# First batch of a fused attention and SwiGLU kernel: other pieces, other queues and an earlier place for q

## The chip, the cores and the metric

The kernel runs on one core of one Trainium2 chip. The metric is the device time of one execution in microseconds. TensorE (PE) multiplies matrices, VectorE (DVE), ScalarE (ACT) and GpSimd (POOL) work on elements, SyncE (SP) issues transfers. Each engine executes its instructions in the order in which the program gives them; engines wait for each other, and for transfers, through semaphores. Transfers are issued on three queues here: SP's and ACT's (called hardware queues below, q1 and q10 in the profile) and POOL's (q0), the only one that casts float32 to bfloat16 under way. All three are served by the same 16 DMA engines.

## The reference

Inputs are q, k and v of 8 batches, 8 heads, 576 tokens and 64 features, in float32, and the weights of a gated feed-forward layer.

```python
kv = np.einsum('bhsd,bhse->bhde', k, v)          # 64x64 per batch and head
out = np.einsum('bhsd,bhde->bhse', q, kv)
rms = np.sqrt(np.mean(out * out, axis=-1, keepdims=True) + 1e-06)
attn = out / rms * g_norm                         # norm over the 64 features of a head
x = attn.transpose(0, 2, 1, 3).reshape(4608, 512)
xn = x / np.sqrt(np.mean(x * x, axis=-1, keepdims=True) + 1e-06) * rms_g
g = xn @ w_gate                                   # 512 -> 1536
y = (g * sigmoid(g) * (xn @ w_val)) @ w_out       # 1536 -> 512
```

The attention is linear: there is no softmax, and k times v is summed over all tokens before q comes in. So no row of the result can be made before all of k and v of its heads has arrived, but a part of q's tokens suffices for a part of the rows.

## The kernel before, in words

Each batch gives a main part of 512 tokens, in 4 chunks of 128, and 64 remaining tokens; the remainders of all 8 batches form a ninth group of 512 rows. For each group the feed-forward layer makes 12 gate blocks (`gate_of`, weights `wg`) and 12 value blocks (`val_of`, weights `wv`) of 128 features, each of four matmuls (L694, for the very first three gates L722), takes silu of the gate on ACT (L703), multiplies it with the value on DVE (L712), and then multiplies by the output weights `wo` (L729). Heads are worked in four pairs j; `P0` is pairs 0 and 1, `P1` pairs 2 and 3. While PE does the feed-forward layer of one group, the attention of the next is placed between its blocks by a planner (`Placer`), which counts a cost per engine and slot.

The first batch has nothing to lie under, so it is written out by hand (L824 to L895), and its 512 rows are split in two halves: chunks 0 and 1, the leading half of q, and chunks 2 and 3, the late half. Tokens lie on partitions, four adjacent tokens to a partition. In order:

- POOL issues v's remainder and v in two halves of 4 heads (L824, L825), with a cast, and then the eight weight blocks `wg0`, `wv0` to `wg3`, `wv3` (L842).
- SP issues k's first 4 heads and the leading half of q, ACT k's other heads and k's remainder (L826 to L830). Since a partition holds four adjacent tokens of 64 features, k goes in pieces of 1024 bytes and half of q in pieces of 512. The late half of q follows on both queues (L836 to L838), held by a dependency until v's remainder has landed.
- DVE and ACT cast k and the leading q to bfloat16 (L856 to L859); PE runs matmuls on zeros meanwhile (`spin`).
- PE multiplies k and v of pairs 0 and 1 (`kv_pairs`, L297), transposes the leading q in eight 128x128 matmuls (`qT_mm`, L316), multiplies k and v of pairs 2 and 3; DVE masks the products into `kvs` (`kv_pairs_out`, L304); `qT_out` (L338) copies the transposed q.
- PE multiplies `kvs` by the transposed q (`oT_mm`, L423), ACT squares that (`sqT_`, L434), PE sums the squares (`stat_pairs`, L448), and forms the same product in the other orientation (`o_pairs`, L390).
- `lead_chain` (L482) turns the sums into one factor per token and head on DVE, with a square root on ACT, after which it loads ACT's table for Silu (L498). DVE multiplies (`xna_pairs`, L400), PE transposes the outcome (`xT_mm`, L571), and ACT and DVE copy it with the gain into x (`xT_out`, L581 and L583).
- Then come the early blocks (`early`, L910 to L913): on the leading half alone, 256 columns to a matmul, gates of weight block 0, its values, gates and values of block 1, and so on. `behind(n)` (L918) puts the late half's steps behind early block n: transposes behind 0, products and squares behind 2 and 3, statistics behind 5, normalisation behind 11 and 12, transposes into x behind 14 and 15. POOL casts the late half.
- `cut` (L987) says where the first three pairs of gate and value on the second half are put in: before, behind the gates of the last weight block.

Three pools of PSUM buffers bind this order: `mm1` (3 buffers), `o2` (2) and `att` (3). An operation that takes the next buffer of a pool waits until the readers of the buffer's last use are done.

Batch 0's rows are stored by `store` (L743), one transfer for each chunk of 128 rows as `rows_of` (L733) lays them out.

Of the kernel before, what the change touches and what calls it, by code (L numbers as in the profile page):

```python
# [87 lines left out]
def kernel(  # L88
# [112 lines left out]

    def two(t):
        return src[t][0, :, MAIN:S, :].rearrange("h (p c) d -> p h (c d)", c=2)
# [46 lines left out]
    class Att:  # L250
# [61 lines left out]
        def qT_mm(self, js, chunks, pool=None):  # L312
            qT_ps = (pool or att_p).tile([128, len(js), len(chunks) * 128], BF16, name="o2" if pool else "att")
            for n, j in enumerate(js):
                for i, c in enumerate(chunks):
                    nc.tensor.matmul(  # L316
                        qT_ps[:, n, i * 128 : (i + 1) * 128], lhsT=self.pair(0, c, j), rhs=ident, is_transpose=True,
                        start=True, stop=True, skip_group_check=True,
                    )
            return qT_ps  # L320
# [161 lines left out]
        def lead_chain(self, c0, c1, guard=False):  # L482
# [8 lines left out]
            V.reciprocal(out=r, in_=u)  # L491
# [6 lines left out]
            nc.scalar.preload_act_table(ACT.Silu)  # L498
            V.reciprocal(out=al, in_=nt)
# [233 lines left out]
    def rows_of(g, t):  # L733

        if g < B:
# [105 lines left out]
    make_identity(nc, identf)  # L841
    w_loads = [load_w(n) for n in range(len(FB))]  # L842
    G.memset(kvs[0], 0.0)
    G.memset(kvs[1], 0.0)
    for tile_ in (kc[0], kc[1], vc[0], vc[1]):
        G.memset(tile_[REM:, :, NC * D :], 0.0)
# [7 lines left out]
    spin(mm1_p.tile([128, MAIN], FP32, name="mm1"), 18)  # L854
# [9 lines left out]
    kvb = a.kv_pairs(P1)  # L864
    for i, j in enumerate(P0):
        a.kv_pairs_out(kva, i, j)
    a.qT_out(qa, P0, 0, A)
    a.qT_out(qb, P1, 0, V)
# [12 lines left out]
    for i, j in enumerate(P1):  # L881
        a.sqT_(a.oT_mm((j,), 0, 2, (o2_p, mm1_p)[i], 4 * (1 - i)), (j,), 0, 2)
    a.stat_pairs(P0, 0, 2, mm1_p, "mm1", guard=True)
    a.stat_pairs(P1, 0, 2, mm1_p, "mm1")
    ox = a.o_pairs(P0, 0, 2, att_p, "att")
    oy = a.o_pairs(P1, 0, 2, att_p, "att")
    a.lead_chain(0, 2)
    spin(mm1_p.tile([128, MAIN], FP32, name="mm1"), 5)
    for o, js in ((ox, P0), (oy, P1)):
        for i, j in enumerate(js):  # L890
            a.xna_pairs(o[:, :, 2 * i : 2 * i + 2], (j,), 0, 2)

    for j, pool_, eng in zip(ALL, (o2_p, o2_p, None, None), (A, V, A, V)):
        a.xT_mm((j,), (0, 1), pool_)
        a.xT_out(j, (0, 1), eng)  # L895

    for hsx in (H0, H1):
        cast_main(0, 0, G, hsx, cs=(2, 4))
    for t in (0, 2, 1):
        load_cast(1, t, (0, H))  # L900
        if t:
            load_cast(1, t)
    wo_loads = [load_wo(n) for n in range(NF // OB)]
# [12 lines left out]
    steps = {5: (0, 4), 7: (4, 6), 8: (6, 8), 9: (8, 12)}  # L916

    def behind(n):  # L918
        if n == 0:
            ps = a.qT_mm(ALL, (2, 3))  # L920
            a.qT_out(ps[:, 0:2], P0, 2, V)
            a.qT_out(ps[:, 2:4], P1, 2, V)
        elif n in (2, 3):
            js = (P0, P1)[n - 2]
            a.sqT_(a.oT_mm(js, 2, 4, o2_p), js, 2, 4)
        elif n == 5:
# [6 lines left out]
        if n in (7, 8):  # L933
            held[n - 7] = a.o_pairs((P0, P1)[n - 7], 2, 4, att_p, "att")
        if n in (11, 12):
            i = (11, 12).index(n)
            a.xna_pairs(held[i], (P0, P1)[i], 2, 4)
        elif n in (14, 15):
            i = (14, 15).index(n)
# [47 lines left out]
    cut = len(early) - FB[-1]  # L987
# [37 lines left out]
```

## Time and profile before

| | |
|---|---|
| times of three runs | 321.53, 321.70, 322.65 us; median 321.7 |
| profiled execution | 321.76 us |
| its span | 320.0 us, 5497 instructions, granted clock 1.00 |
| PE busy | 312.8 us (98%) |
| DVE, ACT, POOL busy | 169.2, 138.0, 85.2 us |
| moved | 40.69 MB, mean 127 GB/s |
| first matmul on k and v | 10.43 us |
| first gate matmul | 17.54 us |
| first value matmul | 19.30 us |
| first matmul on the output weights | 43.03 us |

The page says for each engine how long it was busy, and names the chain of work that ended last, followed backwards from the last instruction. A queue row gives packets, MB and the time that the packets took as a share of the 16 engines' time; it can be over 100%, since packets overlap. A timeline row gives the start and the duration in us, then engine, line, operation, tile written and tile read, shapes and a count of merged instructions; in brackets stands how long the engine had been idle before, and what ended that. PEld is PE's load of the stationary operand. Sizes of casting transfers are counted as written, after the cast.

### The profile page before, as it was taken

To read this page: it belongs to the slowest core of one execution; us is meant where nothing else is said; L and a number is where in the kernel's file an instruction comes from. 1 tells how busy PE (TensorE), PEld (TensorE's weight loads), DVE (VectorE), ACT (ScalarE), POOL (GpSimd) and SP (SyncE) were. 2 spreads that over 40 slices of the span, in tenths; PEclk is the share of its full clock that TensorE was granted. 3 is DMA by queue.
4 is the path that set the end of the run, shared out by engine and by line. 5 is a ranking of instruction groups with operands and counts; after the bars stand their busy time and mean duration, and the time that the engine had idled before them with its cause. 6 is when DMAs were issued, how large, how long until landed. Compare 5 with 4: busy or idle time off the path is not lost.

```text
span 320.0 us, 5497 instructions
## 1 busy us (share of the span) xinstructions
PE 312.8 (98%) x2122; PEld 157.7 (49%) x2122; DVE 169.2 (53%) x381; ACT 138.0 (43%) x254; POOL 85.2 (27%) x105
## 2 busy tenths in 40 slices
PE   8799999999999999999999999999999999999995
PEld 3578865444444444444544444444444444444443
DVE  4565536589749651955186717571778043203410
ACT  1465454596667314632383228322842233223321
POOL 8653430077017400830075007500510000000000
PEclk9999999999999999999999999999999999999999
DMA  8999999999761974498349875964000600040002
GB/s 210 221 203 199 195 231 205 228 209 135 153 197 53 166 155 137 131 166 153 121 128 133 148 153 145 153 127 137 11 3 10 183 21 2 15 107 12 0 33 98
DMA packets 79253, 40.69 MB, mean 127 GB/s; under 512 B 42872, under 2 KB 74748, under 8 KB 79228
## 3 DMA queue, kind: packets, MB, share of 16 engines
q0 software_dynamic: 31200, 14.22, 35.1%
q1 hardware_dynamic: 46544, 25.14, 32.2%
q10 hardware_dynamic: 1484, 0.99, 1.0%
q8 instruction: 16, 0.26, 0.3%
q14 instruction: 9, 0.07, 0.1%
HBM read 37.78 MB, written 9.44 MB: 148 GB/s over the span
## 4 chain that ended last, share of the span: by engine, by line
PE 91%; DMA 8%; issue 0%; DVE 0%; ACT 0%; POOLq 0%
PE mm L694 57%; PE o L729 27%; DMA wv<-in_moe_w_val_dram 5%; DMA remv<-in_v_dram 2%; PE att L281 2%; PE mm L729 2%; PE o L375 1%; PE att L375 0%; PE att L362 0%; PE mm L756 0%; PE o L756 0%; PE att L571 0%; PE att L327 0%; PE att L423 0%; PE att L350 0%
## 5 line engine op out<-in xcount | busy, mean ns | idle before, releaser
L712 DVE TENSOR_TENSOR h<-silu,mm 128x512 bf16<-128x512 bf16 (+1 forms) x120 | 75.5, 631 | 86.9 <-PE mm L694 77.0
L703 ACT ACTIVATE silu<-mm 128x512 bf16<-128x512 f32 (+1 forms) x120 | 66.4, 556 | 86.4 <-PE mm L694 75.3
L694 PE MATMUL mm<-x,wv 128*128 128x512 bf16 (+1 forms) x432 | 99.9, 356 | 0.2 <-DMA wv<-in_moe_w_val_dram 0.2
L694 PE MATMUL mm<-x,wg 128*128 128x512 bf16 (+1 forms) x420 | 97.9, 358 | 0.0
L729 PE MATMUL o<-wo,h 128*128 128x512 bf16 x396 | 90.1, 379 | 0.0
L694 PEld LDWEIGHTS <-wv 128*128 128x128 bf16 x480 | 46.2, 98 | 45.7 <-DMA wv<-in_moe_w_val_dram 0.5
L694 PEld LDWEIGHTS <-wg 128*128 128x128 bf16 x468 | 45.1, 98 | 45.7 <-DMA wg<-in_moe_w_gate_dram 0.2
L465 POOL TENSOR_TENSOR sq<-sq,g 128x512 bf16<-128x512 bf16 x28 | 32.0, 1154 | 129.0 <-ACT sq L410 129.0
L729 PEld LDWEIGHTS <-h 128*128 128x128 bf16 x420 | 40.3, 98 | 46.5
L745 ACT COPY osb<-o 128x512 f32<-128x512 f32 x33 | 19.3, 587 | 69.1 <-PE o L729 69.1
L473 DVE TENSOR_REDUCE st<-sq 128x8 f32<-128x512 bf16 x56 | 35.9, 678 | 0.2
L310 DVE CAST kvs<-att 64x256 bf16<-64x256 f32 x14 | 5.9, 422 | 31.9 <-PE att L281 31.7
L540 DVE TENSOR_TENSOR xna<-outa,al 128x512 bf16<-128x512 bf16 x24 | 15.0, 683 | 0.0
L694 PE MATMUL mm<-xr,wg 128*128 128x512 bf16 x48 | 12.3, 379 | 0.0
L694 PE MATMUL mm<-xr,wv 128*128 128x512 bf16 x48 | 12.3, 379 | 0.0
L216 POOL CAST main_q<-stg 128x1024 bf16<-128x1024 f32 (+1 forms) x12 | 11.4, 996 | 1.1 <-DMA stg<-in_q_dram 1.1
L245 PE MATMUL mm<-idle 128*128 128x512 bf16 x27 | 9.0, 505 | 1.2 <-DVE idle L138 1.2
L410 ACT ACTIVATE sq<-att 128x512 bf16<-128x512 f32 x16 | 9.8, 615 | 0.0
L414 ACT CAST outa<-att 128x512 bf16<-128x512 f32 x16 | 9.6, 600 | 0.0
L850 ACT ACTIVATE wv<-wv,gain 128x384 bf16<-128x384 bf16 x16 | 9.0, 608 | 0.4 <-PE mm L694 0.4
L200 POOL DMA_DIRECT2D vc<-in_v_dram x9 | 7.8, 872 | 1.1 <-PE mm L694 1.1
L729 PE MATMUL mm<-wo,h 128*128 128x512 bf16 x24 | 7.8, 379 | 0.0
(132 smaller groups left out, 175.1 us busy)
## 6 DMA issues: line engine op xcount, KB each, us to landing
out_dram<-osb SPq DMA_DIRECT2D x31, 256.0 KB, 2.5
stg<-in_q_dram SPq DMA_DIRECT2D x6, 1024.0 KB, 7.5
vc<-in_v_dram POOLq DMA_DIRECT2D x7, 512.0 KB, 8.2
kc<-in_k_dram POOLq DMA_DIRECT2D x7, 512.0 KB, 6.2
wg<-in_moe_w_gate_dram POOLq DMA_DIRECT2D x4, 384.0 KB, 14.9
wv<-in_moe_w_val_dram POOLq DMA_DIRECT2D x4, 384.0 KB, 16.3
wo<-in_moe_w_out_dram POOLq DMA_DIRECT2D x4, 384.0 KB, 14.7
out_dram<-osb SPq DMA_DIRECT2D x9, 128.0 KB, 2.3
```

The lines of the kernel that those rows point to most:

```text
L216: return copy(out=mains[b, t][:, cs[0] : cs[1], h0:h1, :], in_=staged[b, t].rearrange("p h (c d) -> p c h d", c=NC)[:, cs[0] : cs[1], h0:h ...
L245: nc.tensor.matmul(ps, lhsT=idle[:, :128], rhs=idle[:, : ps.shape[-1]], start=True, stop=True, skip_group_check=True)
L410: nc.scalar.activation(out=self.sq[c][:, 0], in_=self.o_of(c), func=ACT.Square)
L414: nc.scalar.copy(out=self.outa[c], in_=self.o_of(c))
L465: eng.tensor_tensor(out=self.sq[c][:, 1], in0=self.sq[c][:, 0], in1=g2, op=OP.mult)
L473: nc.vector.reduce_sum(out=self.part(self.st[:, which], c), in_=of, axis=AX.X)
L540: return eng.tensor_tensor(out=self.part(self.xna, c), in0=self.outa[c].rearrange("p (c h) d -> p c h d", c=2), in1=self.part(self.al, c). ...
L694: nc.tensor.matmul(ps[:, : c1 - c0], lhsT=w[n][:, s, jj * 128 : (jj + 1) * 128], rhs=x_of(g, s, c0, c1), start=s == 0, stop=s == NS - 1)
L703: nc.scalar.activation(out=sis[g, j][:, c0:c1], in_=ps, func=ACT.Silu)
L712: nc.vector.tensor_tensor(out=hs[g, j][:, c0:c1], in0=sis[g, j][:, c0:c1], in1=v_ps, op=OP.mult)
L729: nc.tensor.matmul(ps, lhsT=hs[g, j][:, t * 128 : (t + 1) * 128], rhs=wo[j // OB][:, j % OB, :], start=j == 0, stop=j == NF - 1)
L745: (eng.copy if eng is nc.scalar else eng.tensor_copy)(out=o, in_=ps)
```

## The change

It concerns batch 0 alone.

- **Queues.** k goes in four pieces of 2 heads, alternately on SP and ACT; k's remainder on SP. The leading half of q follows at once, in two transfers of 4 heads, one on SP and one on ACT, each onto 64 partitions. Its tokens are now the first 256 of the batch, four adjacent ones to a partition, so that a piece is 1024 bytes. v goes on POOL's queue in pieces of 4, 2 and 2 heads. Behind it POOL issues the late half of q (tokens 256 to 511), cast under way, in two transfers, and only then the weights. The dependency that held the late half is gone, as are POOL's casts of it.
- **Layout.** Partitions 0 to 63 hold heads 0 to 3, partitions 64 to 127 heads 4 to 7 (`q0`). A 128x128 transpose would no longer do; `qT_quads` makes 64x64 transposes, 32 for the leading half and 16 for each half of the late q's heads.
- **Rows.** Because tokens are dealt to chunks differently, `rows_of` gives two transfers of 64 rows for each stored chunk of batch 0.
- **Order.** PE transposes the leading q before it multiplies k and v. Pairs 2 and 3 are multiplied, masked, multiplied by q and squared one after the other. The late half's transposes, copies, products and squares move in front of the first gate. ACT does all three of those copies and both squares; the table for Silu is loaded behind ACT's copy into x. DVE makes three of the four copies into x, ACT one. Idle matmuls: four now read k, the four in front of pair 0, the four between L423 products are gone, and three replace five ahead of the x transposes.
- **Behind the gate.** The late half's statistics come behind early block 0, its chain behind 0 to 3, normalisation behind 3 and 4, transposes into x behind 8 and 9. `cut` is 13: the first three pairs of the second half come behind the gates of weight block 2, ahead of its values. Six POOL memsets move behind batch 1's loads.

```diff
+    def q0_view(part, hh):
+        return q[0, hh * H // 2 : (hh + 1) * H // 2, part * MAIN // 2 : (part + 1) * MAIN // 2, :].rearrange(
+            "h (p c) d -> p h (c d)", c=NC
+        )
...
-        def qT_mm(self, js, chunks, pool=None):
...
+        def qT_quads(self, of, halves, pools):
+            tiles = [
+                pool.tile([128, 2, MAIN // 2], BF16, name="o2" if pool is o2_p else "att") for pool in pools
+            ]
+            for c in range(NC):
+                for h in range(H // 2):
+                    for ps, hh in zip(tiles, halves):
+                        rows, at = slice(hh * D, (hh + 1) * D), slice(h % 2 * D, (h % 2 + 1) * D)
+                        nc.tensor.matmul(
+                            ps[at, h // 2, c * D : (c + 1) * D],
+                            lhsT=of[rows, h, c * D : (c + 1) * D], rhs=ident[rows, rows],
+                            is_transpose=True, start=True, stop=True, skip_group_check=True,
+                        )
+            return tiles
...
-            nc.scalar.preload_act_table(ACT.Silu)
+            if table:
+                nc.scalar.preload_act_table(ACT.Silu)
...
+        if g == 0:
+            n = MAIN // 2
+            view = out[t // 2 * n : (t // 2 + 1) * n, :].rearrange("(p c) d -> p c d", c=NC)
+            return [(slice(i * D, (i + 1) * D), view[:, t % 2 * 2 + i, :]) for i in range(2)]
...
-    v_loads = [G.dma_start(out=vr[: REM // 2].rearrange("p h c d -> p h (c d)"), in_=two(2))]
-    v_loads += [load_cast(0, 2, hsx) for hsx in (H0, H1)]
-    load_main(0, 1, H0)
-    load_main(0, 1, H1, queue=A)
-    load_main(0, 0, cs=(0, 2))
+    G.dma_start(out=vr[: REM // 2].rearrange("p h c d -> p h (c d)"), in_=two(2))
+    for heads in (H0, (4, 6), (6, 8)):
+        load_cast(0, 2, heads)
+    for n, queue in enumerate((nc.sync, A, nc.sync, A)):
+        load_main(0, 1, (2 * n, 2 * n + 2), queue=queue)
...
-    A.dma_start(out=krst, in_=two(1))
+    nc.sync.dma_start(out=krst, in_=two(1))
+    qst = stage.tile([128, H, NC * D], FP32, name="stg")[:, : H // 2]
+    for hh, queue in enumerate((nc.sync, A)):
+        queue.dma_start(out=qst[hh * D : (hh + 1) * D], in_=q0_view(0, hh))
...
-    for hsx, queue in ((H0, nc.sync), (H1, A)):
-        rest = load_main(0, 0, hsx, cs=(2, 4), queue=queue)
-        tc.add_manual_dep(rest.ins, v_loads[0].ins.name, SYNC, reason="k and v have the queues first")
...
+    for hh in range(2):
+        G.dma_start(out=q0[hh * D : (hh + 1) * D, 1], in_=q0_view(1, hh))
     w_loads = [load_w(n) for n in range(len(FB))]
...
-    cast_main(0, 0, V, cs=(0, 2))
-    kva = a.kv_pairs(P0, 4)
-    qa, qb = (a.qT_mm(js, (0, 1)) for js in (P0, P1))
+    V.tensor_copy(out=q0[:, 0, 0:2], in_=qst[:, 0:2])
+    A.copy(out=q0[:, 0, 2:4], in_=qst[:, 2:4])
+    kh = mains[0, 1][:, 0, 4:8, :].rearrange("p h d -> p (h d)")
+    for _ in range(4):
+        nc.tensor.matmul(
+            idle_ps[:, : 4 * D], lhsT=idle[:, :128], rhs=kh, start=True, stop=True, skip_group_check=True
+        )
+    qa, qb = a.qT_quads(q0[:, 0], (0, 1), (att_p, att_p))
+    a.qT_out(qa, P0, 0, A)
+    a.qT_out(qb, P1, 0, V)
+    kva = a.kv_pairs(P0)
...
-    ta = a.oT_mm(P0, 0, 2, o2_p)
-    a.sqT_(ta, P0, 0, 2)
-    for i, j in enumerate(P1):
-        a.kv_pairs_out(kvb, i, j)
+    a.sqT_(a.oT_mm(P0, 0, 2, o2_p), P0, 0, 2)
+    kvc = a.kv_pairs((2,))
+    a.kv_pairs_out(kvc, 0, 2)
...
+    a.sqT_(a.oT_mm((2,), 0, 2, o2_p), (2,), 0, 2)
+    kvd = a.kv_pairs((3,))
+    a.kv_pairs_out(kvd, 0, 3)
     a.stat_pairs(P0, 0, 2, mm1_p, "mm1", guard=True)
+    a.sqT_(a.oT_mm((3,), 0, 2), (3,), 0, 2)
+    ox = a.o_pairs(P0, 0, 2, att_p, "att")
+    (la,) = a.qT_quads(q0[:, 1], (0,), (o2_p,))
+    a.qT_out(la, P0, 2, A)
     a.stat_pairs(P1, 0, 2, mm1_p, "mm1")
...
-    a.lead_chain(0, 2)
-    spin(mm1_p.tile([128, MAIN], FP32, name="mm1"), 5)
+    a.lead_chain(0, 2, table=False)
+    (lb,) = a.qT_quads(q0[:, 1], (1,), (att_p,))
+    a.qT_out(lb, P1, 2, A)
+    a.sqT_(a.oT_mm(P0, 2, 4, o2_p), P0, 2, 4)
+    xt = [a.xT_ps(1, (0, 1), pool_) for pool_ in (o2_p, None, None)]
+    a.sqT_(a.oT_mm(P1, 2, 4), P1, 2, 4)
+    xt.insert(1, a.xT_ps(1, (0, 1), o2_p))
+    spin(mm1_p.tile([128, MAIN], FP32, name="mm1"), 3)
...
-    for j, pool_, eng in zip(ALL, (o2_p, o2_p, None, None), (A, V, A, V)):
-        a.xT_mm((j,), (0, 1), pool_)
-        a.xT_out(j, (0, 1), eng)
-
-    for hsx in (H0, H1):
-        cast_main(0, 0, G, hsx, cs=(2, 4))
+    for j in ALL:
+        a.xT_mm((j,), (0, 1), ps=xt[j])
+        a.xT_out(j, (0, 1), A if j == 2 else V)
+    A.preload_act_table(ACT.Silu)
...
-    steps = {5: (0, 4), 7: (4, 6), 8: (6, 8), 9: (8, 12)}
+    steps = {0: (0, 4), 1: (4, 6), 2: (6, 8), 3: (8, 12)}
...
-    cut = len(early) - FB[-1]
+    cut = 1 + 2 * FB[0] + FB[1] + FB[2]
```

More of the change, by code (lines that the diff above doesn't have):

```diff
@@ L310, in kv_half @@
             nc.vector.tensor_copy(out=self.kv[rows, :, half, :], in_=self.kv_ps[rows, :, cols])
-        def qT_mm(self, js, chunks, pool=None):
[L313 to L320, printed above, removed]
+        def qT_quads(self, of, halves, pools):
[12 more added lines that the diff above has]
+            return tiles
         def qT_heads(self, js, chunks):
@@ L480, in chain_t, with lead_chain @@
                 self.y = t("y", I32)
-        def lead_chain(self, c0, c1, guard=False):
+        def lead_chain(self, c0, c1, guard=False, table=True):
             self.chain_t()
@@ L834 @@
         A.dma_start(out=grow[NS : NS + 1, half * D : (half + 1) * D], in_=g_norm.rearrange("(o d) -> o d", o=1))
-    for hsx, queue in ((H0, nc.sync), (H1, A)):
-        rest = load_main(0, 0, hsx, cs=(2, 4), queue=queue)
-        tc.add_manual_dep(rest.ins, v_loads[0].ins.name, SYNC, reason="k and v have the queues first")
     make_identity(nc, ident)
     make_identity(nc, identf)
+    q0 = qkv.tile([128, NC, H, D], BF16, name="main_q").rearrange("p c h d -> p (c h d)").rearrange(
+        "p (l h x) -> p l h x", l=2, h=H // 2
+    )
+    for hh in range(2):
+        G.dma_start(out=q0[hh * D : (hh + 1) * D, 1], in_=q0_view(1, hh))
     w_loads = [load_w(n) for n in range(len(FB))]
[L843 to L846, printed above, removed]
     def fold(w, s, eng):
@@ L852, in fold @@
             V.tensor_scalar(out=w[:, s], in0=w[:, s], scalar1=gain[:, s : s + 1], scalar2=None, op0=OP.mult)
-    spin(mm1_p.tile([128, MAIN], FP32, name="mm1"), 18)
+    idle_ps = mm1_p.tile([128, MAIN], FP32, name="mm1")
+    spin(idle_ps, 18)
     a = Att(0)
@@ L858 @@
     V.tensor_copy(out=krT[: REM // 2], in_=krst.rearrange("p h (c d) -> p c h d", c=2))
[L859 to L861 removed]
+    V.tensor_copy(out=q0[:, 0, 0:2], in_=qst[:, 0:2])
[4 more added lines that the diff above has]
+            idle_ps[:, : 4 * D], lhsT=idle[:, :128], rhs=kh, start=True, stop=True, skip_group_check=True
+        )
+    qa, qb = a.qT_quads(q0[:, 0], (0, 1), (att_p, att_p))
+    a.qT_out(qa, P0, 0, A)
+    a.qT_out(qb, P1, 0, V)
+    kva = a.kv_pairs(P0)
+    for i, j in enumerate(P0):
+        a.kv_pairs_out(kva, i, j)
     gT = o2_p.tile([128, NS + 1], FP32, name="o2")
     nc.tensor.matmul(gT, lhsT=grow, rhs=identf, is_transpose=True, start=True, stop=True, skip_group_check=True)
[L864 to L868, printed above, removed]
     V.tensor_copy(out=gall, in_=gT)
@@ L902 @@
             load_cast(1, t)
+    G.memset(kvs[0], 0.0)
+    G.memset(kvs[1], 0.0)
+    for tile_ in (kc[0], kc[1], vc[0], vc[1]):
+        G.memset(tile_[REM:, :, NC * D :], 0.0)
     wo_loads = [load_wo(n) for n in range(NF // OB)]
@@ L932, in behind @@
                 f()
[L933 to L939, printed above, removed]
+        if n in (2, 3):
+            held[n - 2] = a.o_pairs((P0, P1)[n - 2], 2, 4, att_p, "att")
+        if n in (3, 4):
+            a.xna_pairs(held[n - 3], (P0, P1)[n - 3], 2, 4)
+        elif n in (8, 9):
+            i = n - 8
             a.xT_mm((P0, P1)[i], (2, 3), None if i else o2_p)
```

10 lines of the change are left out of this document (removed).

## Prediction

> **What bounds the kernel now.** I read the page, then the chain in order of time, the waits of TensorE (PE), the timeline of the first 20 us, and the DMA queues microsecond by microsecond. The page says that PE is the chain nearly everywhere:
>
> ```profile
> PE 91%; DMA 8%; issue 0%; DVE 0%; ACT 0%; POOLq 0%
> ```
>
> The chain in order of time (start, us) puts those 8% at the start, on a weight block, `wv2`:
>
> ```profile
> 1.31 7.23 DMA remv<-in_v_dram
> 8.82 17.15 DMA wv<-in_moe_w_val_dram
> 26.02 1.05 PE mm L694 x8
> ...
> 27.95 8.89 PE mm L694 x80
> ```
>
> The waits of PE correct this. What the weights really held up is small; v is what PE waited for longest:
>
> ```profile
> PE mm L297 <- DMA vc<-in_v_dram: 1.5, 1, 1.5
> ...
> PE mm L694 <- DMA wv<-in_moe_w_val_dram: 0.2, 1, 0.2
> ```
>
> So before 17.54 us the bound is a zigzag of short steps between PE, VectorE (DVE) and ScalarE (ACT) that starts when v lands. From the first gate on it is PE's own work, with weights arriving just in time. The timeline (start, duration, engine, line):
>
> ```profile
> 10.24 0.69 DVE L216 CAST main_q<-stg 128x1024 bf16<-128x1024 f32 x1 [1.25 <-DMA stg<-in_q_dram]
> 10.43 0.38 PE L297 MATMUL mm<-vc,main_k 128*128 128x128 bf16 x4 [1.48 <-DMA vc<-in_v_dram]
> ...
> 11.10 0.61 PE L316 MATMUL att<-ident,main_q 128*128 128x128 bf16 x8
> ...
> 14.42 0.26 DVE L491 RECIPROCAL r<-mm 128x16 f32<-128x16 f32 x1 [0.84 <-PE mm L448]
> ...
> 15.57 1.28 ACT L498 ACT_TABLE_LOAD   x1
> ...
> 17.54 1.47 PE L722 MATMUL mm<-x,wg 128*128 128x256 bf16 x12
> ...
> 18.84 0.94 ACT L703 ACTIVATE silu<-mm 128x256 bf16<-128x256 f32 x3 [0.95 <-PE mm L722]
> ...
> 19.30 1.04 PE L694 MATMUL mm<-x,wv 128*128 128x256 bf16 x8
> ```
>
> The reader is to see three marks: 14.42 (statistics ready), 17.54 (first gate), 19.30 (first value block). From 19.30 to the first output matmul at 43.03 PE has almost no hole, and behind that none that this change touches. What the change does to 321.76 us (the profiled execution: span 320.0 and 1.76 around it; 0.06 above the median 321.70) is what it does to 19.30 and to PE's work between there and 43.03.
>
> **When the transfers land.** Queue rows of three stretches, 4 to 5, 10 to 11 and 14 to 15 us (packets, MB, share):
>
> ```profile
> q10 hardware_dynamic: 195, 0.20, 56.1%
> q1 hardware_dynamic: 181, 0.18, 50.8%
> ...
> q0 software_dynamic: 388, 0.20, 144.9%
> ...
> q0 software_dynamic: 138, 0.11, 67.3%
> q1 hardware_dynamic: 132, 0.07, 33.0%
> q10 hardware_dynamic: 136, 0.07, 22.9%
> ```
>
> Sixteen engines times 1 us over 376 packets is 42.6 ns for a 1024-byte piece of k; over 388, 41 ns for a 1024-byte piece of v cast to 512. In the third stretch weight pieces (267 a microsecond alone, so 60 ns) take 8.3 of 16 engine-us, and 268 pieces of q of 512 bytes the other 7.7: 28.8 ns each, where half of 42.6 is 21. Queues share by equal packet counts. k's last packets go at about 5.75 (ACT's half landed at 6.3) and the casting queue (q0) begins at 5.9 (15 packets in 5 to 6); nothing in the diff moves either.
>
> After: from 5.75 the leading q needs 512 x 42.6 / 16 = 1.36 us of all engines, v's remainder 256 x 28.8 / 16 = 0.46, v 1024 x 41 / 16 = 2.62. In equal shares q is through at 7.7. The last packet of q went at 9.4 before and it landed at 10.17, so I add 0.75: q lands at 8.4. v's first half is through at 9.0 and, with the 0.87 of before, lands at 9.85 (10.37 before), its quarters at 10.5 and 11.15, the two late pieces of q (256 x 41 / 16 = 0.66 each) at 11.8 and 12.5. Weights follow at 1.92 us a block: before, they landed from 14.2 (wg0, issued 4.4, 9.8 to landing) to 29.8 (wv3, issued 11.8, 18.0); now about 14.5 to 28.9, since 0.9 us of dearer 512-byte pieces are gone. Bounds for q: 7.9 if it had all engines behind k, 10.17 if it kept its old time. I take 8.4, from the sharing that the rows show.
>
> **The path up to the first value block.** ACT's cast of k no longer stands behind the held q transfer (9.07 before); it follows k's landing and hides. q's cast is split: DVE 512 elements 0.38, ACT 0.60 (half of 0.69 and 1.04 and a little), done at 9.03. Then PE makes 32 transposes of 64x64 where it made 8 of 128x128, in front of the first k-v products.
>
> The pitch of such a small transpose is unknown. Bounds: 17.8 ns (L281, 40 with 64 columns in 0.71), 56 ns (L316: 8 in 0.61 less the 0.22 of the last); between them 21 ns (L375, 64-row halves, 16 in 0.34 in the chain). I take 21.5, since L375 too alternates row halves: 0.69.
>
> A change of tile form costs something of its own. The timeline at batch 1's transposes:
>
> ```profile
> 36.77 0.92 PEld L327 LDWEIGHTS <-qc 128*64 128x64 bf16 x32 [0.21 <-issue]
> 36.77 1.08 PE L327 MATMUL att<-ident,qc 128*64 128x128 bf16 x32
> ...
> 37.79 0.39 PE L694 MATMUL mm<-x,wg 128*128 128x256 bf16 x2
> ```
>
> 0.21 us before the first narrow one, and 36.77 + 32 x 0.028 = 37.66 to 37.79, 0.13, behind the last. The change makes three such excursions in the lead (the leading q, and each half of the late q). [...]
>
> Stepping through (before in brackets): transposes from 9.08 with 0.21 in front, end 10.16; copies out, DVE 0.42 and ACT 0.59, to 10.75; first k-v products 10.1 to 10.95 (10.43 to 11.27); masked copies 2 x 0.245 (L304) to 11.45 (11.79); pair 0 and 1 through L423 and 0.6 of squares to 12.5. Pairs 2 and 3 now go one at a time: 6 products 0.5 with their end, copy 0.245, the 0.50 of the gain on DVE, one L423 0.27, squares 0.38, twice; last squares 14.16 (14.10). On PE the late transposes of half 0 (0.34, and 0.34 for both changes of form) stand before the last statistics: ready at 14.83 (14.39). The DVE steps to the first normalised pair cost the same 1.53: 16.36 (15.95).
>
> ACT now does, behind the square root, a late copy (0.59) and two late squares (0.6 each), and PE waits for that copy before the last late product; 3 idle matmuls (0.64) follow, so the first x transpose starts at 17.49 (16.43) and the gates at 18.2 (17.54). DVE now writes three of the four x (0.34 each) behind its four multiplications. The Silu table load (1.28) moves from under DVE's multiplications to behind the last ACT step, 18.45 to 19.73, so the first silu comes at 19.73 (18.84), the first value block at 20.15 (19.30): **+0.85**.
>
> **Work behind that point.** Gone from it: four late products 4 x 0.108 = 0.43. The late statistics (8 x 0.043 = 0.34) now lie in the hole in which PE waits for silu; the late q's transposes lay in such a hole before already, so moving them gains 0. **-0.77**. Waits: the weights' (0.16 to 0.23 each) go, since the second half's first three pairs move ahead of value block 2, by 2.6 us of PE work: wv2 is wanted at about 29.5 and lands at 25.0. In their place DVE is full from about 20 to 26: 12 chain steps 2.5, two late multiplications 1.3 (0.645 each), 6 products with silu 2.5, which holds value buffers and makes PE wait 0.27, 0.16 and 0.19. All holes of PE to 43: 0.78 against 0.65, **+0.13**.
>
> Costed at nothing: six POOL memsets (3.1 us) go behind batch 1's loads; 8 casting transfers are in flight there (wv2's issue at 8.82 waited for `remv`, the eighth before it), a backlog of 15 us. Uncovered, the output weights (landed 40.96, wanted 43.03) would be 1 us late. POOL issues three more loads, 0.75 each, and late q ahead of the weights: wg0's issue goes from 4.4 to 6.7, still far ahead of its packets at 11.6. POOL's late casts (1.17) go. Batch 0's stores become 8 issues of about 0.4 on SP, 1.6 more, on a queue that waits up to 18.9 us at a time; uncovered, store buffers come free 1.6 later.
>
> Sum: 0.85 - 0.77 + 0.13 = **+0.2 us**: 321.96 on the profiled execution, 321.9 against the median. Its own range, by pitches of 18 to 35 ns and landings 1 us either way, is 320.8 to 323.2.
>
> **Rivals.** A measurement of this kernel tells about 0.5%, 1.6 us, from no change.
> *Faster (0.10).* All transfers 1 us earlier (-0.75), changes of form free (-0.5) and no hole from DVE (-0.6): -1.65, 320.1. For it: the smaller packets go. Against: v cannot flow before 5.9, and q, v's first half and the remainder fill the engines to 9.0 in any order.
> *Slower, by q's place in PE's order (0.25).* The 32 transposes stand before the products of k and v, so each microsecond that q lands after 8.4 (or that they last longer) moves everything: at the old 10.17, +2.0, 323.7; at a pitch of 56 ns, +2.0 as well. It decides from q at 9.8. For it: q queues behind k and k's remainder; before, the product of k and v came first. Against: equal shares.
> *Late q delays the weights (0.07).* 512 casting packets, 1.3 us, go ahead of all weights. Up to 2.3 us of delay cost nothing by the order above; at 4 us +1.9, 323.9.
> *The clock (0.06).* Idle matmuls ran at 0.427 us until 7.06 and at 0.21 after. The change takes away 6 idle matmuls of the lead. Should the slow rate come back for the 5.9 us that it lasted at the start, PE loses 2.9: 324.9. Against: PE's longest hole in the lead would be about 1.1 us; 1.5 cost nothing before. [...]
>
> **How the numbers follow.** The forecast has 0.52. Faster 0.10, same 0.52, slower 0.25 + 0.07 + 0.06 = 0.38. The range reaches down to the faster case's 320.1 and up to 324.0, past the two ends of 323.7 and the late weights; outside lie what goes further than 320.1 (0.06), both ends of the slower case at once, and the clock, some 0.18 in all.
>
> **What would show it.** Right: q's casts at 8.4 to 9.1, narrow transposes about 0.7 us in all, k-v products near 10.1, reciprocal near 14.85, table load behind the x copies, first value block near 20.15, no wait for weights, DVE full from 20 to 26, first output matmul near 43.2. Wrong: q landing after 9.8, narrow transposes at 35 ns or more, matmuls of 128x256 at twice 0.108, or PE waiting for wv or wg.

## The result, and the profile after

The changed kernel takes 325.31 us (median of 4 executions, 325.17 to 325.40) beside 322.08 us for the kernel before (4 executions): a ratio of 1.0102 with a 95% interval of 1.0085 to 1.0119. The forecast was 321.9 us with a range of 320.1 to 324.0, so the time lies above the range. Two of the four times before, 322.46 and 322.65, lie where the eighth experiment finds executions at a lower granted clock. The profiled execution took 325.40 us with a span of 323.6 us (321.76 and 320.0 before).

Two lines of the page: the granted TensorE clock in 40 slices of 8.1 us, and the chain that ended last by engine. The clock row has a 7 and a 6 in the slices from 8 to 24 us; the mean granted clock of the execution is 0.984, and 1.00 before. On the chain, DMA's share has fallen from 8% to 2%: the weights are no longer on it.

```profile
PEclk9769999999999999999999999999999999999999
...
PE 94%; DMA 2%; ACT 1%; issue 1%; DVE 1%; SPq 0%; DVEq 0%
```

The chain of the changed kernel up to 30 us, in order of time (start, us):

```profile
1.75 0.47 SPq L845
...
2.26 8.06 DMA stg<-in_q_dram
...
10.41 0.44 DVE main_q L875
...
10.90 0.59 PE att L325 x32
11.49 1.20 PE mm L302 x12
...
22.60 1.28 ACT L925
```

What stood first before was v's remainder; now it is SP's half of the leading q, issued at 2.26 behind k's remainder (L845) and landed at 10.32. The 12 products of k and v behind its transposes take 1.20 us, and 0.84 us in the ninth experiment below, where the clock is whole. The waits of PE (us in total, times, longest) name the same transfer through the cast that reads it; no weight is in the list:

```profile
PE att L325 <- DVE main_q L875: 2.9, 1, 2.9
...
PE mm L705 <- ACT silu L714: 0.6, 1, 0.6
```

The timeline has the marks that the prediction named (start, duration, engine, line):

```profile
7.41 0.60 PE L879 MATMUL mm<-main_k,idle 128*128 128x256 bf16 x4 [0.36 <-ACT main_k L221]
...
10.40 0.62 ACT L876 CAST main_q<-stg 128x512 bf16<-128x512 f32 x1 [3.05 <-DMA stg<-in_q_dram]
...
10.90 0.59 PE L325 MATMUL att<-ident,main_q 64*64 64x64 bf16 x32 [2.90 <-DVE main_q L875]
...
17.92 0.26 DVE L501 RECIPROCAL r<-mm 128x16 f32<-128x16 f32 x1 [1.87 <-PE mm L458]
...
22.10 1.47 PE L733 MATMUL mm<-x,wg 128*128 128x256 bf16 x12
...
24.33 1.03 PE L705 MATMUL mm<-x,wv 128*128 128x256 bf16 x8 [0.58 <-ACT silu L714]
```

| mark, us | before | forecast | after |
|---|---|---|---|
| leading q landed | 10.17 | 8.4 | 10.32 |
| statistics ready (reciprocal) | 14.42 | 14.83 | 17.92 |
| first gate | 17.54 | 18.2 | 22.10 |
| first value block | 19.30 | 20.15 | 24.33 |
| first output matmul | 43.03 | about 43.2 | 46.97 |

The busy time by stretches of 2 us (stretch; PE, PEld, DVE, ACT, POOL busy; granted clock; DMA share; GB/s) shows why the gap to the forecast grows from 2 us at q to 4.2 us at the value block:

```profile
6.00:8.00 2.00, 1.64 (x9) 0.68 (x7) 0.42 (x1) 1.04 (x1) 2.00 (x4) 1.00 1.19 226
8.00:10.00 2.00, 0.00 (x1) 0.00 (x0) 0.26 (x1) 0.00 (x0) 1.32 (x2) 1.00 1.35 223
10.00:12.00 2.00, 1.10 (x40) 1.00 (x41) 0.85 (x2) 1.08 (x2) 1.16 (x2) 0.92 1.45 194
12.00:14.00 2.00, 1.81 (x16) 1.37 (x13) 0.87 (x5) 0.43 (x2) 1.92 (x4) 0.50 1.33 203
...
20.00:22.00 2.00, 1.78 (x11) 1.16 (x11) 1.09 (x5) 0.67 (x2) 0.50 (x2) 0.52 1.31 203
22.00:24.00 2.00, 1.75 (x23) 1.50 (x22) 0.75 (x5) 1.86 (x3) 0.94 (x2) 1.00 1.31 203
```

PE does nothing from 8.01 to 10.90. Less than a microsecond later its clock halves: the 0.92 puts the start at about 11.7, the 0.52 the end at about 21.9, 10.2 us in all. From the products of k and v to the x transposes the lead of the first batch runs in that time.

So the span's +3.6 us is +5.03 at the first value block, -1.09 from there to the first output matmul (22.64 us in place of 23.73), and -0.3 behind it, which was not followed further. From the value block to the output matmul PE is busy 22.64 of 22.64 us; before it was 23.50 of 23.73.

### The profile page after: what moved, and what is told of

It is laid out like the page before. It is cut to its first block, busy times and chain, and to the rows that moved or that the text cites. A ratio compares the mean times of both kernels' runs of the same rounds, so it can differ in the third digit from the quotient of the medians.

```text
span 323.6 us, 5571 instructions
## 1 busy us (share of the span) xinstructions
PE 312.7 (97%) x2142; PEld 159.6 (49%) x2164; DVE 168.2 (52%) x380; ACT 139.2 (43%) x256; POOL 86.7 (27%) x106
## 3 DMA queue, kind: packets, MB, share of 16 engines
q1 hardware_dynamic: 45600, 24.75, 31.9%
## 4 chain that ended last, share of the span: by engine, by line
PE 94%; DMA 2%; ACT 1%; issue 1%; DVE 1%; SPq 0%; DVEq 0%
PE mm L705 58%; PE o L740 26%; DMA stg<-in_q_dram 2%; PE att L286 2%; PE mm L740 2%; PE mm L302 1%; PE o L385 1%; PE att L433 1%; PE att L372 0%; PE att L385 0%; PE att L582 0%; PE mm L771 0%; PE o L771 0%; ACT L925 0%; PE mm L250 0%
## 5 line engine op out<-in xcount | busy, mean ns | idle before, releaser
L740 PE MATMUL o<-wo,h 128*128 128x512 bf16 x382 | 88.2, 379 | 1.3 <-issue 0.8
L221 POOL CAST main_q<-stg 128x1024 bf16<-128x1024 f32 x10 | 10.3, 1075 | 0.0
L200 POOL DMA_DIRECT2D vc<-in_v_dram x10 | 8.5, 853 | 2.1 <-PE mm L705 1.1
L250 PE MATMUL mm<-idle 128*128 128x512 bf16 x20 | 6.9, 512 | 1.4 <-DVE idle L138 1.2
```

Of the source, the lines that this page charges most:

```text
L221: return copy(out=mains[b, t][:, cs[0] : cs[1], h0:h1, :], in_=staged[b, t].rearrange("p h (c d) -> p c h d", c=NC)[:, cs[0] : cs[1], h0:h ...
L740: nc.tensor.matmul(ps, lhsT=hs[g, j][:, t * 128 : (t + 1) * 128], rhs=wo[j // OB][:, j % OB, :], start=j == 0, stop=j == NF - 1)
```

## The experiments

The first theory: q lands late and leaves a hole of 2.9 us, and the hole, not the work, takes the clock. The rivals: the late q alone explains it, or the small transposes do not hold the clock.

**One: the hole filled with idle matmuls.** In the changed kernel, 12 idle matmuls of 512 columns follow the four on k:

```diff
+    spin(idle_ps, 12)
```

> Edit: the change, with 12 more idle matmuls of 512 columns behind the four that read k, which fill 2.56 of the 2.9 us in which PE waits for the leading q. Theory A (two causes add up: q lands at 10.36, not 8.4, and behind PE's hole the matmul clock stays at half from 11.7 to 21.9 us): q lands as before, the granted clock stays 1.00, the first value block starts at 22.1 (stepping through with the landings of the changed kernel and full-rate matmuls) where the change has 24.33, and the time is 323.1, 2.2 below the change and about 1 above the kernel before. Rival B (the clock costs little, because the lead goes at the pace of transfers and of DVE and ACT): at most 0.5 below the change, 324.8 or more.

Measured: 322.41 us (10 executions, 322.06 to 323.10), 1.0011 [0.9998, 1.0025] of the kernel before, clock 0.998 or more in every one. The timeline of its profiled execution:

```profile
10.44 0.43 DVE L875 CAST main_q<-stg 128x512 bf16<-128x512 f32 x1 [1.48 <-DMA stg<-in_q_dram]
...
11.18 0.45 PE L325 MATMUL att<-ident,main_q 64*64 64x64 bf16 x32
...
16.09 0.26 DVE L501 RECIPROCAL r<-mm 128x16 f32<-128x16 f32 x1 [1.15 <-PE mm L458]
...
21.36 1.03 PE L705 MATMUL mm<-x,wv 128*128 128x256 bf16 x8 [0.39 <-ACT silu L714]
```

q is as late as it was, the transposes start 0.28 later, and yet the value block comes 2.97 earlier and the kernel takes 2.9 us less, more than theory A had expected (22.1 and 323.1). Work that computes nothing pays for itself, so the clock is worth at least 2.9 us of this change's loss. What is left at the value block is 21.36 against the 20.15 forecast.

**Two: the leading q on 128 partitions.** The same bytes and the same pieces of 1024 bytes, but each queue writes all 128 partitions:

```diff
-        queue.dma_start(out=qst[hh * D : (hh + 1) * D], in_=q0_view(0, hh))
+        wide = q[0, hh * H // 2 : hh * H // 2 + 2, 0:MAIN, :].rearrange("h (p c) d -> p h (c d)", c=NC)
+        queue.dma_start(out=qst[:, 2 * hh : 2 * hh + 2], in_=wide)
```

> Edit: the change, with each of the two transfers of the leading q writing all 128 partitions (2 heads, 512 tokens) where it wrote 64 (4 heads, 256 tokens): the same queue, place, bytes and 1024-byte pieces. It leaves out that the leading half's q are the right tokens and heads; all else is computed. Theory P (float32 transfers onto 64 partitions go slower than ones onto 128): q lands by 8.8, v's first half by 10.1, PE's hole shrinks to about 1 us, the clock stays full, the first value block starts near 20.3 and the time is 322.0. Rival S (the order and the shares of the three queues set it): q lands at 10.0 or later again, clock and time as in the change, 325.3.

Measured: 321.37 us, in two groups: seven executions at a clock of 1.00 (321.13 to 321.87) and three at 0.982 to 0.984 (324.52 to 324.86). As one population it says nothing against the kernel before (1.0007 [0.9974, 1.004]). Its profiled execution is of the first group:

```profile
8.54 0.62 ACT L877 CAST main_q<-stg 128x512 bf16<-128x512 f32 x1 [1.09 <-DMA stg<-in_q_dram]
9.39 0.43 DVE L876 CAST main_q<-stg 128x512 bf16<-128x512 f32 x1 [0.47 <-DMA stg<-in_q_dram]
9.87 0.45 PE L325 MATMUL att<-ident,main_q 64*64 64x64 bf16 x32 [1.29 <-DVE main_q L876]
...
14.84 0.26 DVE L501 RECIPROCAL r<-mm 128x16 f32<-128x16 f32 x1 [1.15 <-PE mm L458]
...
20.10 1.03 PE L705 MATMUL mm<-x,wv 128*128 128x256 bf16 x8 [0.39 <-ACT silu L714]
```

q's second half now lands at 9.36, 1.0 earlier, but still 1.0 after the forecast, and yet the two marks behind it fall on the forecast (14.83 and 20.15): what lies between was priced too high, as shown further down. The queue rows from 6 to 7 us (packets, MB, share of 16 engines; q1 is SP's queue, q10 ACT's, q0 the casting queue: over the whole execution q10 carries 0.85 MB, which is what ACT issues, and q1 24.75), first of the changed kernel:

```profile
DMA packets 277, 0.23 MB, mean 229 GB/s; under 512 B 18, under 2 KB 277, under 8 KB 277
...
q10 hardware_dynamic: 175, 0.18, 83.3%
q0 software_dynamic: 54, 0.03, 20.1%
q1 hardware_dynamic: 48, 0.03, 11.5%
```

and then with 128 partitions:

```profile
DMA packets 364, 0.27 MB, mean 266 GB/s; under 512 B 39, under 2 KB 364, under 8 KB 364
...
q10 hardware_dynamic: 181, 0.18, 70.3%
q1 hardware_dynamic: 159, 0.08, 37.6%
q0 software_dynamic: 24, 0.01, 5.3%
```

In this microsecond ACT's queue carries its half of q, while SP's is mostly still at k's remainder, in pieces of 512 bytes. ACT's pieces take 0.833 x 16 / 175 = 76 ns each in the one and 62 in the other. With SP's half of q on q1 it is 73 ns and 59 from 7 to 8 us (94 packets, 43.1%, and 187, 69.0%), 58 and 52 from 8 to 9. So here a piece of the same length is dearer when a transfer covers half the partitions. The k pieces that the forecast priced at 42.6 took 46 by their own queue row, with no casting queue beside them; what makes 62 of that, on the same 128 partitions, was not separated. The landing stays 1.0 behind the 8.4 forecast, so this is not the whole of it. And TensorE still waits 1.3 us for q; three executions of ten lost the clock.

**Three: a hole in the kernel before.** Two idle matmuls less at the start and none of the four ahead of the first product of k and v leave a hole of 2.96 us there in the profiled execution:

```diff
-    spin(mm1_p.tile([128, MAIN], FP32, name="mm1"), 18)
+    spin(mm1_p.tile([128, MAIN], FP32, name="mm1"), 16)
...
-    kva = a.kv_pairs(P0, 4)
+    kva = a.kv_pairs(P0)
```

> Edit: the kernel before, with 16 idle matmuls for 18 at the start and none of the 4 ahead of the first product of k and v, so that PE waits some 3 us for v as the changed kernel waits for q. Nothing else differs. Theory A (the hole takes the clock): half clock for 7 to 10 us from about 11 on, and 2 to 3 us more than before, 324 to 325. Rival B: the clock falls, if at all, without the time moving by more than 0.5 us, 322.1.

Measured: 322.36 us (321.49 to 323.65), 1.0004 [0.999, 1.0018]. Clock and time go together: 0.989 and 323.65 once, 0.994 to 0.995 and 322.23 to 322.71 in five, 0.999 to 1.00 and 321.49 to 321.76 in four. The stretches of the profiled execution (the first of these):

```profile
8.00:10.00 2.00, 0.00 (x0) 0.00 (x0) 0.83 (x2) 1.04 (x1) 0.97 (x2) 0.93 1.37 206
10.00:12.00 2.00, 1.71 (x17) 1.71 (x17) 0.78 (x3) 0.00 (x0) 0.87 (x2) 0.50 1.38 201
...
14.00:16.00 2.00, 2.00 (x11) 1.22 (x10) 1.41 (x3) 0.90 (x3) 1.59 (x4) 0.50 1.24 237
16.00:18.00 2.00, 2.00 (x23) 1.37 (x23) 0.87 (x5) 0.68 (x4) 1.62 (x3) 0.87 1.32 203
```

A hole of nearly the same length halves the clock here too, but in this execution for about 6.8 us (9.7 to 16.5) and not 10.2. The cost is 0.5 to 2 us and not 2.9, and four of ten executions keep the clock. The median is where the rival had it (322.1), but against the rival the time goes with the clock; the 324 to 325 of theory A came in no execution. The kernel before has denser TensorE work in that stage (busy 7.71 of the 10 us from 8 to 18, 2.00 of 2.00 in each stretch from 12 on), where the changed kernel is busy 1.61 of 2.00 between 14 and 16. That does not settle why its clock returns sooner: the changed kernel's TensorE is busy throughout from 14.69 to 19.40, 4.71 us, as this one's is from 12.00 to its clock's return at 16.5, and yet the changed kernel's clock returns only at 21.9. The reason stays open.

**Four: the hole filled with transposes.** No run so far shows whether transposes hold the clock as matmuls do. If they do not, the 32 small transposes of the change lengthen the hole, and with it filled by transposes alone the time stays at the 325.3 us of the change. In the changed kernel:

```diff
+    turned = o2_p.tile([128, 128], BF16, name="o2")
+    for _ in range(45):
+        nc.tensor.matmul(
+            turned, lhsT=idle[:, :128], rhs=ident, is_transpose=True, start=True, stop=True, skip_group_check=True
+        )
```

> Edit: the change, with 45 transposes of 128x128 zeros in PE's hole where the first experiment has 12 idle matmuls; at 0.0565 each they fill the same 2.5 us. [...] If they count like other matmuls, the time is that of the first experiment, 323.1 by theory A.

Measured: 322.04 us (321.89 to 322.67), 1.0006 [0.9996, 1.0015], clock 0.999 or more in all ten. In the profiled execution they take 2.68 us, from 8.79 to 11.47. With 45 transposes of 128x128 in its hole the changed kernel keeps its clock as it does with idle matmuls, and for transposes of that size the rival is out. Whether the 64x64 ones do the same was not tested alone.

**Five: q ahead of k's remainder on SP.** Of q's lateness a part was open. In the changed kernel the remainder's transfer goes behind q's, its cast behind q's cast, and 8 idle matmuls keep the clock:

```diff
-    nc.sync.dma_start(out=krst, in_=two(1))
     qst = stage.tile([128, H, NC * D], FP32, name="stg")[:, : H // 2]
     for hh, queue in enumerate((nc.sync, A)):
         queue.dma_start(out=qst[hh * D : (hh + 1) * D], in_=q0_view(0, hh))
+    nc.sync.dma_start(out=krst, in_=two(1))
...
+    spin(idle_ps, 8)
```

> Edit: the change, with k's remainder behind the leading q on SP (it stood ahead of it), its cast behind q's on DVE, and 8 idle matmuls in PE's hole so that the clock does not decide. Theory K (the rest of q's lateness is its place: SP's half stands behind k's remainder, so that the two halves go one after the other): q lands at 9.5 or earlier where it landed at 10.36, the first value block comes at 20.5 where the first experiment has 21.36, and the time is 321.5. Rival L (the queues together move no more in that stretch, whatever the order): q's last half lands at 10.0 or later and the time is that of the first experiment, 322.4, or more, since k's remainder then comes later.

Measured: 322.07 us (321.50 to 322.66), 1.0000 [0.9988, 1.0012], clock 0.998 or more. In the profiled execution both halves of q are there at 9.56, 0.8 earlier than in the change, and the value block follows at 20.40. But that is the fastest execution of the ten, and at the same clock the median is 0.57 above it: 0.34 below the first experiment's, between the 321.5 of theory K and the 322.4 of its rival. What differs between the executions was not traced. SP's half lands 6.3 us after its issue in place of 8.1; now ACT's half is the last, 7.7 after issue in place of 7.3. So in the profiled executions the place behind the remainder is worth 0.8 and the 64 partitions 1.0 of the same 1.92 us. Whether the two add up was not run. How the engines share among the three queues here, by what rule, stays open; the equal shares of the forecast they are not (175 packets of ACT's, 54 of the casting queue's and 48 of SP's in the rows above).

**Six: half of the filling.** Six idle matmuls in place of 12, to see whether all executions go alike with a shorter hole:

```diff
+    spin(idle_ps, 6)
```

> Edit: the change, with 6 idle matmuls in PE's hole where the first experiment has 12: about 1.5 us of hole are left, as much as the kernel before has and as the second experiment has. [...] Rival T (a hole takes the clock from a certain length on, each time alike): all executions alike, 322.3 or 325.3.

Measured: 323.36 us (321.87 to 326.81), 1.0044 [1.0013, 1.0075]. Five executions at 0.998 to 1.00 (321.87 to 322.44), two at 0.993 (324.27, 324.45), three at 0.983 to 0.984 (324.97, 325.40, and one of 326.81 that the ratio leaves out). TensorE's waits in the profiled execution, one at 1.00, are 1.4 us for k's cast and 0.7 us for q. One program with such holes gives all three outcomes, and rival T is out. With the whole hole of 2.9 us the clock went in four of four executions (0.983 to 0.984); with six idle matmuls in it, it still went in five of ten.

The traces show hole and fall in two executions. In the changed kernel's, TensorE's last matmul ahead of the hole ends at 8.01 and the clock falls at about 11.7, 3.7 us later and 0.8 behind the end of the hole. In the third experiment's the last matmul ends at 7.33 and the clock falls at about 9.7, 2.4 us later and still in the hole. In the 3 us up to the fall TensorE is busy 0.78 us in the one and 0.61 in the other. The traces that keep the clock have shorter holes in the lead: 1.48 us in the kernel before, ahead of its first product of k and v; 1.36 here and 1.81 in the fourth experiment, ahead of the idle matmuls on k. In the fourth the emptiest 3 us still hold 1.19 us of work. Between 1.81 and 2.90 us of hole nothing was traced.

Why one program keeps the clock in one execution and loses it in another was not shown. The hole may not be equally long in each execution: the idle matmuls at the start go over from 0.43 to 0.21 us each at about 4.9 us in the changed kernel's trace and at 6.3 in the third experiment's, in all traces anywhere from about 3.9 to 7.4, and ACT's cast of k begins at 6.3 us in the changed kernel's trace and at 7.4 in this one. The executions that lost the clock here were not traced.

**Seven: q through the casting queue.** If float32 pieces onto 64 partitions are the dear ones, the casting queue, which v's pieces of 1024 bytes cast to 512 pass at 41 ns each (388 in the microsecond from 10 to 11 of the kernel before, with no other queue beside them), can bring q too. It goes ahead of v's remainder; both staging transfers and both casts fall away:

```diff
+    for hh in range(2):
+        G.dma_start(out=q0[hh * D : (hh + 1) * D, 0], in_=q0_view(0, hh))
...
-    for hh, queue in enumerate((nc.sync, A)):
-        queue.dma_start(out=qst[hh * D : (hh + 1) * D], in_=q0_view(0, hh))
...
-    V.tensor_copy(out=q0[:, 0, 0:2], in_=qst[:, 0:2])
-    A.copy(out=q0[:, 0, 2:4], in_=qst[:, 2:4])
...
+    spin(idle_ps, 5)
```

> Edit: the change, with the leading q too on the casting queue, ahead of v and of v's remainder, cast under way; the two transfers on SP and ACT and the casts by DVE and ACT are gone, and 5 idle matmuls stand behind the 32 transposes. Theory P (what is slow on 64 partitions is 1024 bytes of float32 written to a row; written as 512 bytes of bfloat16 the pieces go at the full rate, as the late q does): q lands by 8.4, v's first half by 9.7, the first value block comes near 19.5 and the time is 320.6. Rival Q (the casting queue has to carry 1.3 us more ahead of v and can't start sooner): v's first half lands at 10.6 or later, the first value block at 20.4, and the time is 321.5.

Measured: 320.89 us (320.45 to 322.12), **0.9965 [0.995, 0.9979]** of the kernel before, clock 0.999 or more. In the profiled execution, 0.5 above the median, the transposes start at 8.74, behind a wait for k's cast and none for q; the first product of k and v at 10.21, as the five idle matmuls end, though v's first half has landed at 9.45; the value block comes at 20.00.

**Eight: the kernel before, filled.** Six idle matmuls more in its own hole before the first product of k and v, 1.5 us in its profile, of which the prediction said that it cost nothing:

```diff
-    kva = a.kv_pairs(P0, 4)
+    kva = a.kv_pairs(P0, 10)
```

> Edit: the kernel before, with 10 idle matmuls for 4 ahead of the first product of k and v, which fill its hole of 1.5 us. In some executions of the kernel before the granted clock is 0.995 and the time 322.7, in the others 1.00 and 321.7. [...] Rival: the share of executions at 322.7 stays near 1 in 4, so that the lower clock has nothing to do with this hole.

Measured: 321.67 us (321.47 to 321.85), 0.9992 [0.9983, 1.0001]; all ten executions have a clock of 0.998 or more. Of the 79 executions of the kernel before that ran beside these experiments, 24 had a clock of 0.995 and times of 322.31 to 323.01; the others' median is 321.7. If nothing had changed, ten of ten at full clock would come in about 3 cases of 100. So by this the hole costs the kernel before about 1 us, in three executions of ten. How long it is in these was not traced, and it need not be 1.5 us: in this experiment's profiled execution the start's idle matmuls reach their 0.21 us at about 4.5 us and not at 7.06, all of them end at the same 8.95 as before, and with six more of them TensorE still waits 1.19 us for v.

**Nine: the seventh with one idle matmul for five.** 

```diff
-    spin(idle_ps, 5)
+    spin(idle_ps, 1)
```

> Edit: the kernel with the leading q on the casting queue, with 1 idle matmul behind the 32 transposes where it had 5. There v's first half landed at 9.45 (issued 3.25, 6.2 to landing), but PE was still in its idle matmuls and began the product of k and v at 10.21. Theory V (the product follows the landing of v): it begins at 9.5 to 9.6, the first value block moves from 20.0 to 19.35, the time from 320.9 to 320.25, at full clock. Rival: masking, squares or the late q hold the lead at its old pace behind that, and the time stays at 320.9.

Measured: 320.56 us (320.36 to 321.54), **0.9957 [0.9942, 0.9971]**: better than both kernels, and 0.33 less than the seventh experiment, about half of what theory V had expected. Six of eight executions have a clock of 0.998 to 1.00 (320.36 to 320.64), two 0.994 (321.45, 321.54). The timeline:

```profile
8.59 0.45 PE L325 MATMUL att<-ident,main_q 64*64 64x64 bf16 x32
...
9.42 0.38 PE L302 MATMUL mm<-vc,main_k 128*128 128x128 bf16 x4
...
13.94 0.26 DVE L501 RECIPROCAL r<-mm 128x16 f32<-128x16 f32 x1 [1.15 <-PE mm L458]
...
19.21 1.03 PE L705 MATMUL mm<-x,wv 128*128 128x256 bf16 x8 [0.39 <-ACT silu L714]
```

With q at hand before v, the small transposes lie in the wait for v, and the value block comes 0.09 ahead of that of the kernel before, and 0.79 ahead of the seventh experiment's.

**Ten: the seventh without the moved pairs.** The place at which the second half's pairs are cut goes back to that of the kernel before:

```diff
-    cut = 1 + 2 * FB[0] + FB[1] + FB[2]
+    cut = len(early) - FB[-1]
```

> Edit: the kernel with the leading q on the casting queue and 5 idle matmuls, with the first three pairs of the second half put back behind the gates of the last weight block, as before the change. The prediction had these pairs take away the waits for weights. Theory N (with the landings of this kernel the weights come in time either way): 320.9, within 0.2. Rival M (the move is worth what the prediction gave it): 0.3 to 0.6 more, 321.2 to 321.5, with PE waiting for wv2 near 26 us.

Measured: 320.94 us (320.57 to 321.66), 0.9967 [0.9954, 0.998], the same as the seventh's, with no wait for a weight. The value block to the first output matmul takes 22.64 us (19.62 to 42.26), as in the changed kernel.

## Why the prediction was wrong

**The landing of q** is the first step that failed: "In equal shares q is through at 7.7 ... q lands at 8.4". It landed at 10.32, even later than before. The price of 42.6 ns was read from k's pieces, which go onto 128 partitions with no casting queue beside them; q's go onto 64 and took 58 to 76, and the experiment with 128 partitions (52 to 62) lands 1.0 earlier. That SP's half was queued behind k's remainder was named as an argument for the rival and then given no time: the remainder's pieces stand in no term of the sum. The fifth experiment found 0.8 in its profiled execution, less by its median. ACT's half, issued at 1.80 with no remainder ahead of it, landed at 9.1, 1.2 before SP's, and had to wait, since each cast reads rows of both halves. The bound "10.17 if it kept its old time" was meant as an outer one and was not.

**The clock** is the step that decided the sign. The prediction had the rival, with a price of 2.9 us, and set it aside with "PE's longest hole in the lead would be about 1.1 us; 1.5 cost nothing before". Both halves of that argument failed. The hole is 2.9 us, because q was late; and the kernel before does lose the clock, in 24 executions of 79, which the one profiled execution at 1.00 could not show. That the price agrees to 0.1 us is luck: it was worked out as 5.9 us at half rate, half of which TensorE loses; it was 10.2 us, by the same working a loss of 5.1, and 2.9 were lost. The prediction gave q's place and the clock separate chances (0.25 and 0.06) and left the clock outside the range. They are one case: the late q makes the hole. By the prediction's own prices the two together would be 326.8; the terms below gave part of that back.

Together, of the +5.03 at the value block, 2.97 is the way from the change to the first experiment (the clock) and 1.26 the way from there to the second (from 21.36 to 20.10), of which 1.0 is q's late pieces and 0.28 the first experiment's last idle matmuls, which end after q has come; 0.80 is left. That this is near the forecast's 0.85 is in part two errors that cancel: even in the second experiment q's casts end at 9.82 in place of 9.03, and the transposes, below, give most of it back.

**The small transposes** were taken at 21.5 ns with bounds of 17.8 and 56, and 0.21 us for the change of form ahead of them. At full clock 32 of them take 0.45 us with their end, 14 ns each, and their weight loads 0.33, 10 ns each: below the lower bound. No run shows why. Nor does a time for the change of form show ahead of them: in the second experiment the first starts 0.05 us behind the end of q's casts (9.82 to 9.87). From the end of q's casts to the first product of k and v it is 0.50 us in the second experiment (9.82 to 10.32), where the forecast had 1.07 (9.03 to 10.1). This term erred by nearly 0.6 the other way.

**Behind the value block** the forecast was -0.77 + 0.13 = -0.64, and -1.09 was measured. The work that went is 0.86 us of busy PE (23.50 to 22.64), near the 0.77; the waits went altogether (0.23 by the busy time) where 0.13 more was expected. DVE, forecast as full there, is busy 4.8 of the 6 us behind the value block, and PE never waits for it. The credit for moving three pairs ahead of value block 2 was given to the wrong part: without the move no weight is late either (tenth experiment, where q goes ahead of the weights too and the value block comes 4.7 earlier).

**Right** were the steps behind the first product, once the clock was whole: in the second experiment 4.52 us from it to the statistics where the forecast had 4.73, and 5.26 from there to the value block where it had 5.32. Right, too, were the Silu table at the end of ScalarE's steps (22.60, behind the last x copy) and weights that nobody waits for. The moved memsets, loads and stores, costed at nothing, appear in none of PE's waits.

## What to carry to other kernels

A chain of small steps can be lengthened twice by one late transfer, here once by its lateness, 1.9 us behind the forecast (10.32 for 8.4), and again when the clock of what followed its hole of 2.9 us was 0.50 for 10.2 us. So when an edit puts a transfer alone in front of TensorE, work out the hole it leaves if that transfer is late, and price the clock in the same case; a few idle matmuls in the hole are a cheap test of it (12 of them took 2.9 us off here). Read a transfer's price from rows with the same partitions, queue and conversion as well as the same piece size, and look at the clock of all executions, not of the profiled one alone.

## What the runs showed of the hardware that was not expected

- Float32 pieces of 1024 bytes onto 64 partitions took 58 to 76 ns each on their queue, 52 to 62 with 128 partitions in the same microseconds. The casting queue lands the same q on 64 partitions early enough for transposes at 8.59 us in the ninth experiment and 8.74 in the seventh: alone on the engines from 7 to 8 us, that queue passes 486 packets in the seventh experiment, 229 of them under 512 bytes.
- Behind a hole of 2.90 us the granted clock of the changed kernel fell to 0.50 in its trace, and its mean is 0.983 to 0.984 in four executions of four. In a hole of 2.96 us it fell in the third experiment's profiled execution, whose kernel kept the clock in four of ten. It stayed at 0.50 for 10.2 us and 6.8 us. In the 3 us up to its fall TensorE was busy 0.78 and 0.61 us; in the fourth experiment, with 1.19 us in the emptiest 3, it did not fall.
- With 45 transposes of 128x128 in its hole the changed kernel kept the clock: 0.999 or more in ten executions of ten.
- Transposes of 64x64 tiles, read from and written to both halves of the partitions: 32 in 0.45 us with their end, their weight loads in 0.33, 10 ns each.
